# The flag of the weights behind the sum of the gate logits, three more low parts on ScalarE and Pool, and sums at the end moved forward

## The chip, the cores and the metric

The kernel runs on 1 core of one Trainium2 chip. The metric is the device time of one execution in microseconds: 616.71 us before the change (median of 3 runs, 616.56 to 619.94).

## What is computed

Clustered attention (2 batches, 8 heads, 768 tokens, 64 dimensions; a query sees only keys of its own cluster), then two mixture-of-experts layers over its 1536 tokens of 512 dimensions, each with 8 experts of 1024 hidden units and one expert per token. The first layer has a capacity per expert, the second an output gate on top. The layers, cut to what matters here:

```python
logits = x @ w_gate
e_idx = np.argmax(logits, axis=1)                    # one expert per token
gate_w = softmax(logits)[arange(N), e_idx]
eom = 1.0 / (1.0 + np.exp(-(x @ w_output_gate)))     # layer 2 alone
for e in range(E):
    mask = e_idx == e                                # layer 1: at most `capacity` tokens
    h = np.maximum(x[mask] @ w1[e], 0.0)
    out[mask] = gate_w[mask, None] * eom[mask, e, None] * (h @ w2[e])
```

## The kernel before

One program runs attention (0 to about 290 us), layer 1 (to about 460 us) and layer 2. The experts of a layer are ordered by how many tokens they have, and each place in this order (a rank) has a fixed number of rows: 192, 304, 208, 200, 192, 176, 168, 120 in layer 1. The work is cut into units, one per rank, and two for a layer's first rank: units 0 to 8 are layer 1, units 9 to 17 layer 2 (unit 9 has 256 rows, unit 17 has 88). What a unit does is written in the class MoE; `run` (L1079) puts the instructions of all engines into one order by hand, and each engine works its own queue in that order.

A unit: its tokens are gathered by an indirect DMA from Pool (`gather`), transposed on TensorE (`entry`), multiplied by the first weights (`mm1`, 8 steps f) and by the second (`mm2`, 4 steps d). Products are made from pairs of float16: a value is a high part and a low part, and three products are added. For the weights ScalarE makes the high part `wh` from the loaded `raw`, and VectorE the low part `wl` (`split`, two halves for each chunk of 1 MB; the finished low part frees `raw` for the next load, which SyncE issues). For the hidden layer ScalarE makes `hh` from the PSUM tile, and VectorE the low part `hl`. The table `FP` (L751) names the steps f of a unit in which `hl` is made otherwise: ScalarE runs once more over the PSUM tile into `hr` in float32, and Pool subtracts `hh` from it. For more than 128 rows there is one buffer `hr`, for up to 128 there are two halves. The PSUM tiles of `mm1` and `mm2` rotate over three banks. In some units of layer 2 (unit 9 among them) `mm2_by_token` multiplies the other way round (`pz`, L1000).

Each pass of VectorE over weights also sums its result into `fl`; the sum over a rank is `flt`, and a matmul with ones spreads it (`rank_ok`, L1035), from which VectorE makes `okr`: 1 if all weights are finite. `okr` marks a rank's tokens as valid.

The exit of a unit runs beside the next unit, one step of a Python generator ahead of each f or d. In layer 1 (`exit1`, L1657): the first step sums the gate logits of the unit on TensorE (`pq`), then the flag (`rank_ok` into another column of the same PSUM tile `pq`), then ScalarE copies `pq` to `lt`. The second step multiplies `lt` by `sel` into the last columns of `pq` and transposes the unit's output (`back`, tile `pyo`). The third (in unit 8, the last of the layer, still the second) makes `vbk` from `okr` on Pool and the logits `lg` on VectorE. The tile `yt`, into which ScalarE copies the results of `mm2`, has one buffer: the next unit's first copy waits for the transposes `pyo` of the unit before. The exits of several units form a group; at its last unit `routed` (L1726) chooses experts, gates and places, writes the tokens for layer 2, and in the last group builds the order of the experts and the gather indices of layer 2.

At the very end VectorE adds up the lost tokens of both layers (`lost1`, `lost2`), a matmul with ones spreads the sum, and with the counts beyond the ranks (`nov1`, `nov2`) it gives the number of rounds of a general path, which is 0 here. A register load and a branch on it end the program (L1911 to L1924).

Of the kernel before, what the change touches and what calls it, by code (L numbers as in the profile page):

```python
# [8 lines left out]
F32 = mybir.dt.float32  # L9
# [3 lines left out]
ALU = mybir.AluOpType  # L13
AX = mybir.AxisListType
# [710 lines left out]
class MoE:  # L725
# [23 lines left out]
    FX = 1  # L749
    FB = 0  # L750
    FP = {0: (2, 3, 4, 5, 6, 7), 5: (1, 3, 5), 7: (5, 7), 8: (1, 2, 5, 6), 9: (3, 4)}  # L751
    FY = 7
    SA = (1, 1, 1, 0, 1, 0, 0, 0, 0, 1, 1, 1)
    SB = (1, 1, 1, 1, 1, 1, 1, 1, 1, 1, 1, 1)
# [554 lines left out]
def tile_kernel(tc, q, k, v, centroids, wg1, w11, w12, cap_in, wg2, wog2, w21, w22, out,  # L1309
                prof1=(192, 304, 208, 200, 192, 176, 168, 120), prof2=(392, 272, 224, 192, 160, 128, 120, 88),  # L1310
                head1=128, head2=256, cut2=5, by_token=(0, 3, 5), group1=((0, 1), (2, 3), (4, 5), (6, 7, 8)), seq1=(1, 2, 3, 4, 5, 6, 7), seq2=(1, 6, 2, 5, 3, 4, 7), dbg=None):
    nc = tc.nc
    P = 128
    B, NP, _, S = q.shape
    NT, DM = out.shape
    E = wg1.shape[1]
# [6 lines left out]
    A1, A2 = (sum(len(t) for _, t in u) for u in (units1, units2))  # L1323
    S1 = sum(prof1)
    with ExitStack() as ctx:
        ctx.enter_context(tc.manual_schedule())
        const = ctx.enter_context(tc.tile_pool(name="const", bufs=1))
# [4 lines left out]
        R = Routing(tc, const, E)  # L1332
# [15 lines left out]
        lost1, lost2, tok2 = c32("lost1", A1), c32("lost2", A2), c32("tok2", A2)  # L1348
# [4 lines left out]
        if True:  # L1353
# [68 lines left out]
            keep = {}  # L1422
# [206 lines left out]
            s2 = Stage(units2, x2d, w21, w22, sws[1])  # L1629
            M = MoE(tc, mctx, ident, R, XW, DM, (s1, s2), ps_t)  # L1630
# [9 lines left out]
        def back(ys):  # L1640
            ps = []
            for i, yT in enumerate(ys):
                n = yT.shape[2]
                p = M.ps_t.tile([P, 512], F32, tag="t", name="pyo")
                for c in range(4):
                    nc.tensor.transpose(p[:n, c * P:(c + 1) * P], yT[:, c, :], ident)  # L1646
                ps.append(p)
            return ps

        fin = {}  # L1650
# [6 lines left out]
        def exit1(unit, ys):  # L1657

            group = of[id(unit)]
            ns, gs, u = unit.tiles, unit.gt, unit.u  # L1660
            t0 = group[0].first
            T = sum(len(x.tiles) for x in group)
# [10 lines left out]
            pq = M.ps_g.tile([P, 512], F32, tag="g", name="pq")  # L1673
            for c in range(4):
                nc.tensor.matmul(pq[32 * c:32 * c + 32, :N], wgc[:, c, :], unit.y[:, c, :N], start=True, stop=True)
            M.rank_ok(unit, pq[:, 511 - 2 * E * len(ns):])
            lt = M.sm.tile([P, max(prof1)], F32, tag="e1lt", name="lt", bufs=1)
            nc.scalar.copy(lt[:, :N], pq[:, :N])
            yield
# [2 lines left out]
            for i, n in enumerate(ns):  # L1682
                nc.tensor.matmul(pg[:n, 2 * E * i:2 * E * (i + 1)], lt[:, o:o + n], sel, start=True, stop=True)
                o += n
            xo = [M.xo.tile([P, XW], F32, tag="xo", name="xo") for _ in ns]
            xos += zip(xo, ns)
            ps = back(ys)
# [190 lines left out]
        def exit2(unit, ys):  # L1878
            t0, ns, gs, u = unit.first, unit.tiles, unit.gt, unit.u
# [6 lines left out]
                nc.gpsimd.memset(ls, 0.0)  # L1886
            tk = M.sm.tile([P, T], I32, tag="tk", name="tk")
            M.rank_ok(unit)
            ps = back(ys)
            if unit.xo:  # L1890
                nc.vector.tensor_reduce(ls, unit.ls, axis=AX.X, op=ALU.add)
# [16 lines left out]
        s2.units[-1].last = True  # L1908
        M.run(task)
        lim1, nov1, lim2, nov2 = keep["lim"], keep["nov"], fin["lim"], fin["nov"]  # L1910
        nov = const.tile([P, 1], F32, name="nov")  # L1911
        nl = const.tile([P, 2], F32, name="nl")
        nc.vector.tensor_reduce(nl[:, 0:1], lost1, axis=AX.X, op=ALU.add)
        nc.vector.tensor_reduce(nl[:, 1:2], lost2, axis=AX.X, op=ALU.add)
        nc.vector.tensor_tensor(nl[:, 0:1], nl[:, 0:1], nl[:, 1:2], op=ALU.add)
        pc = M.ps_g.tile([P, 512], F32, tag="g", name="plost")
        nc.tensor.matmul(pc[:, :1], R.ones, nl[:, 0:1], start=True, stop=True)
        nc.vector.tensor_tensor(nov, nov1, nov2, op=ALU.add)
        nc.vector.tensor_tensor(nov, nov, pc[:, :1], op=ALU.add)
        novi = const.tile([P, 1], I32, name="novi")  # L1920
        nc.vector.tensor_scalar_add(novi, nov, 127.0)
        nc.vector.tensor_single_scalar(novi, novi, 7, op=ALU.arith_shift_right)
        mctx.close()
        nt = nc.values_load(novi[0:1, 0:1], min_val=0, max_val=NT // P)  # L1924
# [47 lines left out]
```

## Time and profile before

| | us |
|---|---|
| median of 3 runs (lowest, highest) | 616.71 (616.56, 619.94) |
| the profiled execution | 615.39 |
| its span, first to last instruction | 613.5 |
| TensorE (PE) busy | 565.1 (92%) |
| TensorE weight loads (PEld) busy | 466.1 (76%) |
| VectorE (DVE) busy | 466.1 (76%) |
| ScalarE (ACT) busy | 421.3 (69%) |
| GpSimd (POOL) busy | 215.4 (35%) |

The profile shows one execution of the program. Times are microseconds from the start of the span, and L with a number is a line of the kernel. An instruction's idle time before it is given in brackets with the instruction that ended the wait; idle time of an engine that isn't the bottleneck costs nothing by itself. The chain that ended last is followed back from the last instruction, at each step to what released it.

### The profile page before, as it was taken

To read this page: it belongs to the slowest core of one execution; us is meant where nothing else is said; L and a number is where in the kernel's file an instruction comes from. 1 tells how busy PE (TensorE), PEld (TensorE's weight loads), DVE (VectorE), ACT (ScalarE), POOL (GpSimd) and SP (SyncE) were. 2 spreads that over 40 slices of the span, in tenths; PEclk is the share of its full clock that TensorE was granted. 3 is DMA by queue.
4 is the path that set the end of the run, shared out by engine and by line. 5 is a ranking of instruction groups with operands and counts; after the bars stand their busy time and mean duration, and the time that the engine had idled before them with its cause. 6 is when DMAs were issued, how large, how long until landed. Compare 5 with 4: busy or idle time off the path is not lost.

```text
span 613.5 us, 14527 instructions
## 1 busy us (share of the span) xinstructions
PE 565.1 (92%) x5428; PEld 466.1 (76%) x5428; DVE 466.1 (76%) x1186; ACT 421.3 (69%) x901; POOL 215.4 (35%) x426
## 2 busy tenths in 40 slices
PE   6899999998999998988899999997998999999993
PEld 2666767676767676657778998996887988999992
DVE  5867686778989676868586788789778666989881
ACT  4766666776676668963585787875864576969781
POOL 8702020202341110115634355624624523263441
PEclk9899999999999999999899999999999999999997
DMA  5879482747409881522466765976973657999930
GB/s 145 212 217 283 123 176 88 169 110 153 146 22 241 247 242 35 178 70 107 150 219 236 244 208 201 306 246 194 326 234 89 235 181 245 316 305 312 318 114 21
DMA packets 75920, 117.55 MB, mean 192 GB/s; under 512 B 10906, under 2 KB 43802, under 8 KB 75843
## 3 DMA queue, kind: packets, MB, share of 16 engines
q1 hardware_dynamic: 72419, 106.76, 58.3%
q0 software_dynamic: 3264, 9.72, 4.7%
q8 instruction: 45, 0.74, 0.5%
q14 instruction: 32, 0.26, 0.1%
q10 hardware_dynamic: 160, 0.07, 0.0%
HBM read 84.28 MB, written 12.87 MB: 158 GB/s over the span
## 4 chain that ended last, share of the span: by engine, by line
PE 61%; DVE 17%; ACT 12%; issue 4%; DMA 3%; SPq 1%; ACTq 0%; POOL 0%; DVEq 0%
PE ph L950 15%; PE py L1025 13%; PE av L280 9%; PE pss L238 7%; PE ppt L268 6%; PE pz L1000 3%; DVE nm L246 3%; DVE wl L847 3%; ACT wh L840 3%; ACT pe L254 2%; PE pyo L1646 2%; PE pxt L927 2%; ACT pt L270 1%; ACT xo L1700 1%; DVE hl L962 1%
## 5 line engine op out<-in xcount | busy, mean ns | idle before, releaser
L847 DVE SCALAR_TENSOR_TENSOR wl<-raw,sw,wh 128x1024 f16<-128x1024 f32 x128 | 163.5, 1284 | 17.9 <-ACT wh L840 16.8
L840 ACT ACTIVATE wh<-raw,sw 128x1024 f16<-128x1024 f32 x128 | 146.0, 1148 | 2.5 <-DMA x<-ot 2.4
L246 DVE TENSOR_REDUCE nm<-pss 128x1 f32<-128x768 f32 x96 | 91.5, 953 | 41.2 <-PE pss L238 37.6
L254 ACT ACTIVATE pe<-pss,nm 128x768 f32<-128x768 f32 x96 | 87.1, 907 | 24.2 <-DVE nm L246 24.2
L950 PEld LDWEIGHTS <-wh 128*128 128x128 f16 x1152 | 87.7, 99 | 15.4 <-issue 10.9
L238 PE MATMUL pss<-y,x 128*128 128x384 f32 x384 | 93.6, 365 | 4.8 <-ACT pe L254 3.2
L268 PE MATMUL ppt<-ident,pe 128*128 128x128 f32 x576 | 80.4, 275 | 3.3 <-ACT pt L270 1.4
L238 PEld LDWEIGHTS pss<-y,x 128*128 128x128 f32 x384 | 63.2, 190 | 25.2 <-issue 13.2
L270 ACT COPY pt<-ppt 128x384 f32<-128x384 f32 x128 | 57.9, 482 | 29.4 <-PE ppt L268 29.1
L268 PEld LDWEIGHTS ppt<-ident,pe 128*128 128x128 f32 x576 | 69.2, 142 | 8.9 <-ACT pt L270 2.3
L1025 PEld LDWEIGHTS <-wh 128*128 128x128 f16 x960 | 73.2, 100 | 3.4
L950 PE MATMUL ph<-xh,wh 128*128 128x192 f16 (+14 forms) x576 | 67.2, 240 | 8.6 <-DVE hl L962 6.2
L280 PE MATMUL av<-pt,v 128*64 128x384 f32 x384 | 68.8, 494 | 0.0
L950 PE MATMUL ph<-xl,wh 128*128 128x192 f16 (+14 forms) x576 | 67.3, 240 | 0.2 <-issue 0.2
L950 PE MATMUL ph<-xh,wl 128*128 128x192 f16 (+14 forms) x576 | 67.3, 240 | 0.0
L952 ACT ACTIVATE hh<-ph 128x128 f16<-128x128 f32 (+14 forms) x144 | 44.5, 315 | 27.1 <-PE ph L950 25.8
L962 DVE SCALAR_TENSOR_TENSOR hl<-ph,hh 128x192 f16<-128x192 f32 (+14 forms) x127 | 41.1, 336 | 24.4 <-ACT hh L952 22.8
L1025 PE MATMUL py<-hh,wh 128*128 128x192 f16 (+13 forms) x480 | 47.3, 241 | 0.5 <-ACT hh L952 0.3
L1025 PE MATMUL py<-hl,wh 128*128 128x192 f16 (+13 forms) x480 | 46.9, 240 | 0.2 <-DVE hl L962 0.2
L950 PEld LDWEIGHTS <-wl 128*128 128x128 f16 x576 | 45.5, 99 | 1.9
L1025 PE MATMUL py<-hh,wl 128*128 128x192 f16 (+13 forms) x480 | 46.7, 241 | 0.0
L280 PEld LDWEIGHTS av<-pt,v 128*64 128x64 f32 x384 | 24.8, 136 | 28.4 <-issue 28.1
(326 smaller groups left out, 865.3 us busy)
## 6 DMA issues: line engine op xcount, KB each, us to landing
raw<-in_moe_w SPq DMA_DIRECT2D x64, 1024.0 KB, 5.9
y<-kh SPq DMA_DIRECT2D x31, 192.0 KB, 4.0
x<-qh SPq DMA_DIRECT2D x30, 192.0 KB, 4.6
q<-in_q SPq DMA_DIRECT2D x8, 384.0 KB, 4.8
k<-in_k SPq DMA_DIRECT2D x8, 384.0 KB, 5.0
x<-ql SPq DMA_DIRECT2D x16, 192.0 KB, 3.3
v<-in_v SPq DMA_DIRECT2D x8, 384.0 KB
out<-zt SPq DMA_DIRECT2D x1, 3072.0 KB
```

The lines of the kernel that those rows point to most:

```text
L238: nc.tensor.matmul(p[:, hf, :W], xx[:, c * P:(c + 1) * P], yy[:, hf * W:(hf + 1) * W], start=a, stop=o)
L246: nc.vector.tensor_reduce(nm, p[:, :, :W], axis=AX.XY, op=ALU.max, negate=True)
L254: nc.scalar.activation(pe, p[:, :, :W], AF.Exp, bias=d["nm", c, j], scale=1.0, accum_out=d["sm"][:, c, j:j + 1])
L268: nc.tensor.transpose(p[:, kc * P:(kc + 1) * P], pe[:, kh, kc * P:(kc + 1) * P], ident)
L270: eng(pt[:, kh * HALF:(kh + 1) * HALF, (c % HALF) * P:(c % HALF + 1) * P], p.rearrange("p (a b) -> p a b", a=HALF))
L280: nc.tensor.matmul(p[j * D:(j + 1) * D, :W], d["v"][:, j, kc, :], d["pt", hf, j][:, kc, :], start=(kc == 0), stop=(kc == C - 1))
L840: nc.scalar.activation(hi[:, :, s], x[:, :, s], AF.Copy, scale=sw)
L847: nc.vector.scalar_tensor_tensor(lo[:, :, s], x[:, :, s], sw, hi[:, :, s], op0=ALU.mult, op1=ALU.subtract, accum_out=fl)
L950: nc.tensor.matmul(p[:, :N], w[:, c, fs], x[:, c, :N], start=(k == 0), stop=(k == 11))
L952: nc.scalar.activation(hh[:, f, :N], p[:, :N], AF.Relu)
L962: nc.vector.scalar_tensor_tensor(hl[:, f, :N], p[:, :N], 0.0, hh[:, f, :N], op0=ALU.max, op1=ALU.subtract)
L1025: nc.tensor.matmul(p[:, :N], w[:, f, s], x[:, f, :N], start=(k == 0), stop=(k == 23))
```

## The change

Three edits. In `exit1` the call of `rank_ok` moves from the first step (ahead of the copy `lt`) to the second (behind the products with `sel`). In `FP` unit 9 gets the steps 5, 6 and 7 in addition to 3 and 4. At the end, the sums over `lost1` and over all columns of `lost2` but the last, their sum, and the sum of both counts and 127 move into the last unit's exit, right behind its `rank_ok`; the last column of `lost2` is added by a second matmul into the same PSUM element.

```diff
--- before.py
+++ after.py
@@ -748,7 +748,7 @@
               (1, 1, 0, 1, 0, 1, 0, 1, 1, 1, 0, 1))
     FX = 1
     FB = 0
-    FP = {0: (2, 3, 4, 5, 6, 7), 5: (1, 3, 5), 7: (5, 7), 8: (1, 2, 5, 6), 9: (3, 4)}
+    FP = {0: (2, 3, 4, 5, 6, 7), 5: (1, 3, 5), 7: (5, 7), 8: (1, 2, 5, 6), 9: (3, 4, 5, 6, 7)}
     FY = 7
     SA = (1, 1, 1, 0, 1, 0, 0, 0, 0, 1, 1, 1)
     SB = (1, 1, 1, 1, 1, 1, 1, 1, 1, 1, 1, 1)
@@ -1673,7 +1673,6 @@
             pq = M.ps_g.tile([P, 512], F32, tag="g", name="pq")
             for c in range(4):
                 nc.tensor.matmul(pq[32 * c:32 * c + 32, :N], wgc[:, c, :], unit.y[:, c, :N], start=True, stop=True)
-            M.rank_ok(unit, pq[:, 511 - 2 * E * len(ns):])
             lt = M.sm.tile([P, max(prof1)], F32, tag="e1lt", name="lt", bufs=1)
             nc.scalar.copy(lt[:, :N], pq[:, :N])
             yield
@@ -1682,6 +1681,8 @@
             for i, n in enumerate(ns):
                 nc.tensor.matmul(pg[:n, 2 * E * i:2 * E * (i + 1)], lt[:, o:o + n], sel, start=True, stop=True)
                 o += n
+
+            M.rank_ok(unit, pq[:, 511 - 2 * E * len(ns):])
             xo = [M.xo.tile([P, XW], F32, tag="xo", name="xo") for _ in ns]
             xos += zip(xo, ns)
             ps = back(ys)
@@ -1886,6 +1887,15 @@
                 nc.gpsimd.memset(ls, 0.0)
             tk = M.sm.tile([P, T], I32, tag="tk", name="tk")
             M.rank_ok(unit)
+            if unit is s2.units[-1]:
+                assert T == 1
+                nl = const.tile([P, 2], F32, name="nl")
+                nov = fin["sum"] = const.tile([P, 1], F32, name="nov")
+                nc.vector.tensor_reduce(nl[:, 0:1], lost1, axis=AX.X, op=ALU.add)
+                nc.vector.tensor_reduce(nl[:, 1:2], lost2[:, :t0], axis=AX.X, op=ALU.add)
+                nc.vector.tensor_tensor(nl[:, 0:1], nl[:, 0:1], nl[:, 1:2], op=ALU.add)
+                nc.vector.scalar_tensor_tensor(nov, keep["nov"], 127.0, fin["nov"], op0=ALU.add, op1=ALU.add)
+                fin["nl"] = nl
             ps = back(ys)
             if unit.xo:
                 nc.vector.tensor_reduce(ls, unit.ls, axis=AX.X, op=ALU.add)
@@ -1908,17 +1918,11 @@
         s2.units[-1].last = True
         M.run(task)
         lim1, nov1, lim2, nov2 = keep["lim"], keep["nov"], fin["lim"], fin["nov"]
-        nov = const.tile([P, 1], F32, name="nov")
-        nl = const.tile([P, 2], F32, name="nl")
-        nc.vector.tensor_reduce(nl[:, 0:1], lost1, axis=AX.X, op=ALU.add)
-        nc.vector.tensor_reduce(nl[:, 1:2], lost2, axis=AX.X, op=ALU.add)
-        nc.vector.tensor_tensor(nl[:, 0:1], nl[:, 0:1], nl[:, 1:2], op=ALU.add)
         pc = M.ps_g.tile([P, 512], F32, tag="g", name="plost")
-        nc.tensor.matmul(pc[:, :1], R.ones, nl[:, 0:1], start=True, stop=True)
-        nc.vector.tensor_tensor(nov, nov1, nov2, op=ALU.add)
-        nc.vector.tensor_tensor(nov, nov, pc[:, :1], op=ALU.add)
+        nc.tensor.matmul(pc[:, :1], R.ones, fin["nl"][:, 0:1], start=True, stop=False)
+        nc.tensor.matmul(pc[:, :1], R.ones, lost2[:, A2 - 1:A2], start=False, stop=True)
         novi = const.tile([P, 1], I32, name="novi")
-        nc.vector.tensor_scalar_add(novi, nov, 127.0)
+        nc.vector.tensor_tensor(novi, fin["sum"], pc[:, :1], op=ALU.add)
         nc.vector.tensor_single_scalar(novi, novi, 7, op=ALU.arith_shift_right)
         mctx.close()
         nt = nc.values_load(novi[0:1, 0:1], min_val=0, max_val=NT // P)
```

## Rows read from the trace of the kernel before

**Rows 1.** The page's first line: span and instructions of the execution.

```profile
span 613.5 us, 14527 instructions
```

**Rows 2.** Busy time by stretch: us, engines (x instructions), granted clock, DMA share, GB/s.

```profile
...
410.00:430.00 20.00, 15.85 (x194) 14.58 (x192) 17.84 (x62) 13.47 (x28) 8.22 (x16) 0.96 0.61 185
550.00:570.00 20.00, 20.00 (x238) 19.06 (x236) 18.93 (x45) 18.87 (x38) 9.45 (x15) 1.00 0.93 307
```

**Rows 3.** Waits, ScalarE and TensorE, 290 to 460: us in all, times, longest.

```profile
...
ACT lt L1678 <- DVE okr L1044: 10.7, 8, 3.8
...
PE pq L1683 <- ACT lt L1678: 2.1, 3, 1.8
```

**Rows 4.** Timeline, 419 to 436: start, us, engine, line, instruction [idle before <- releaser].

```profile
...
426.98 0.31 ACT L1678 COPY lt<-pq 128x176 f32<-128x176 f32 x1 [3.76 <-DVE okr L1044]
...
427.34 0.59 PE L1683 MATMUL pq<-sel,lt 128*128 128x16 f32 x4 [1.77 <-ACT lt L1678]
...
429.35 0.30 ACT L1027 COPY yt<-py 128x168 f32<-128x168 f32 x1 [1.02 <-PE pyo L1646]
...
434.12 0.17 DVE L1710 TENSOR_SCALAR am<-am 128x2 f32<-128x2 f32 x1 [2.09 <-ACT xo L1700]
```

**Rows 5.** Busy time by stretches of 2 us behind that wait.

```profile
...
428.00:430.00 2.00, 2.00 (x15) 1.82 (x15) 1.90 (x9) 0.98 (x3) 0.38 (x1) 0.61 0.53 66
430.00:432.00 2.00, 2.00 (x18) 2.00 (x16) 1.88 (x7) 0.70 (x1) 1.70 (x2) 0.54 1.04 398
```

**Rows 6.** Timeline of Pool, 402 to 448, and one row of ScalarE.

```profile
...
420.56 0.50 POOL L960 TENSOR_TENSOR hl<-hr,hh 128x168 f16<-128x168 f32 x1
423.30 1.22 POOL L960 TENSOR_TENSOR hl<-hr,hh 128x168 f16<-128x168 f32 x1 [2.24 <-ACT hr L959]
...
438.41 0.76 POOL L908 TENSOR_SCALAR vb<-xg 128x1 f32<-128x1 f32 x1 [0.59 <-DMA xg<-x2d,idx2a]
...
442.12 0.30 ACT L959 ACTIVATE hr<-ph 128x120 f32<-128x120 f32 x1
```

**Rows 7.** Chain that ended last, 362 to 408: start, us, engine, tile, line.

```profile
...
363.34 0.31 PE pq L1042 x2
```

**Rows 8.** Timeline, 443 to 456.

```profile
...
444.46 0.21 PE L1025 MATMUL py<-hh,wh 128*128 128x120 f16 x1 [0.34 <-ACT hh L952]
...
454.31 0.26 ACT L1678 COPY lt<-pq 128x120 f32<-128x120 f32 x1 [0.56 <-DVE okr L1044]
...
455.92 0.42 DVE L962 SCALAR_TENSOR_TENSOR hl<-ph,hh 128x256 f16<-128x256 f32 x1 [0.45 <-ACT hh L952]
```

**Rows 9.** Timeline, 459 to 482: the head of layer 2.

```profile
...
462.60 0.38 ACT L959 ACTIVATE hr<-ph 128x256 f32<-128x256 f32 x1 [0.57 <-POOL hl L960]
...
464.15 0.66 POOL L960 TENSOR_TENSOR hl<-hr,hh 128x256 f16<-128x256 f32 x1
...
465.69 0.28 PE L616 MATMUL ppos<-av,rv 128*128 128x32 f16 x5
...
467.03 1.06 DVE L962 SCALAR_TENSOR_TENSOR hl<-ph,hh 128x256 f16<-128x256 f32 x3
467.49 1.03 PE L1000 MATMUL pz<-wh,hh 128*128 128x256 f16 x8 [1.52 <-DVE hl L962]
```

**Rows 10.** Chain that ended last, 440 to 482.

```profile
...
467.49 8.02 PE pz L1000 x72
```

**Rows 11.** Timeline, 592 to 614: the end.

```profile
...
603.62 0.16 DVE L1891 TENSOR_REDUCE ls<-ls 128x1 f32<-128x4 f32 x1 [0.21 <-ACT xo L977]
...
604.25 0.16 DVE L1055 TENSOR_TENSOR lost<-vb,vld 128x1 f32<-128x1 f32 x1
...
604.86 0.38 PE L1917 MATMUL plost<-nl,ones 128*128 128x1 f32 x2 [1.65 <-DVE nl L1915]
605.28 0.16 DVE L1919 TENSOR_TENSOR nov<-nov,plost 128x1 f32<-128x1 f32 x1 [0.41 <-PE plost L1917]
605.48 0.15 DVE L1921 TENSOR_SCALAR novi<-nov 128x1 int32<-128x1 f32 x1
```

## The prediction

> **What bounds the kernel now.** I read the page first: one core, one span of 613.5 us [rows 1]; with what lies around it the profiled execution took 615.39 us, and the median of the three timed runs is 616.71 us, 1.3 us more. My sum is made against the profiled execution and then subtracted from the median. A measurement of this kernel tells about 1% (6 us) from no change.
>
> Next I read the table of busy times by stretch [rows 2]. In the second layer TensorE is busy in every moment (20.00 of 20 us between 550 and 570): what is won before it shifts the rest as a whole, as long as weights keep up, and no conversion of weights on ScalarE waits for a DMA there. Late in layer 1 it is otherwise: from 410 to 430 TensorE works 15.85 of 20 us, VectorE 17.84, and TensorE's granted clock averages 0.96. So layer 1 and its seam to layer 2 are where small edits can count.
>
> Third the table of waits [rows 3]. ScalarE's copy `lt` of the gate logits (L1678) waited 10.7 us for VectorE's `okr` (L1044), in all 8 units that carry a flag, though `lt` doesn't use `okr`: both read the PSUM tile `pq`, and the two reads run one after the other in program order. `okr` stands in VectorE's queue behind low parts (`wl`) and `hl`, so the copy inherits VectorE's lateness. But TensorE waited for `lt` only three times, 2.1 us in all and 1.8 of it at one place. Most of the 10.7 us is idle time of an engine that would wait for something else next. The size of the effect has to be read place by place.
>
> **Edit 1: the flag behind the sum.** Removed: `okr` ahead of `lt`. Added: nothing; the flag's two matmul passes and `okr` move one step later, behind `sel`. On TensorE the flag now stands between `sel` and the transposes `pyo`; on VectorE `okr` moves behind one low part; on Pool `vbk`, which reads `okr`, follows later, in front of two small copies per tile. No DMA moves.
>
> The large place is unit 6's exit [rows 4]. `lt` starts at 426.98 after 3.76 us of waiting, `sel` at 427.34 after TensorE idled 1.77, and the next `yt` copy only at 429.35, since it may overwrite `yt` only after `pyo`. Behind that idle time the granted clock fell to 0.61 and 0.54 in two stretches of 2 us [rows 5], the lower of TensorE's two levels (1.2 against 2.4 GHz) for most of them: 0.39 x 2 + 0.46 x 2 = 1.7 us of TensorE's time. Without the wait TensorE is 1.77 + 1.7 = 3.5 us ahead. The chain then goes over ScalarE and VectorE, and there `am` at 434.12 shows what is late next: VectorE idled only 2.09 us before it, its own low parts ending at 432.03. So at most 2.1 us come through, not 3.5.
>
> Not all of that need stay. The gathered tokens for the first unit of layer 2 land by their own clock: Pool got the second tile at 438.41 after waiting 0.59 us for its DMA [rows 6], and the index that starts this gather doesn't come earlier. Behind it in Pool's queue stand that tile's two scalings and two `hl` subtractions of unit 8, and these free the buffer `hr` that ScalarE takes again at 442.12. Shifted by 2.1 us ScalarE would want it at 440.0; Pool is done at about 438.41 + 0.76 + 0.3 + 2 x 0.50 = 440.5. That gives back 0.5 us: I take 1.6 us, with 0 and 2.1 as bounds.
>
> At the other seven places the flag itself has to be priced: 0.31 us of TensorE [rows 7]. Where the chain runs over TensorE both before and after (the exits at 342, 363 and 404 us), 0.31 us leave one side of the main matmuls and return on the other: 0. Where TensorE stalls in the main matmuls anyway, the flag was free ahead of that stall and is paid behind it. That is so at 444.46, where the last `hh` is 0.34 us late [rows 8]: -0.3 us. At the exits near 302 and 387 the two remaining waits of [rows 3] (0.3 us together) go and 0.31 us each comes: -0.3 together, or -0.2 where a little of the flag stays hidden; I take -0.2. The last exit gains: `lt` had waited 0.56 us there with a weight conversion and a `hh` queued behind it on ScalarE, and VectorE waited 0.45 us for that `hh` at 455.92 [rows 8], right ahead of the routing of the last group. 0.45 less the pass of `okr`, now ahead of the logits (about 0.15 us): +0.3 us. Edit 1: 1.6 - 0.3 - 0.2 + 0.3 = 1.4 us; bounds -0.9 (0 at the large place and at the last exit, flags paid in full) and 2.3 (2.1 + 0.45 - 0.3).
>
> **Edit 2: f = 5, 6, 7 of unit 9 by ScalarE and Pool.** Removed from VectorE: three `hl`, 1.06 us at 467.03 [rows 9], behind the whole loading order of layer 2. The first `pz` matmul takes the PSUM bank of f = 5 and waited 1.52 us for the first of these. Added: three `hr` on ScalarE (0.38 us each) and three subtractions on Pool (0.66 us each), and one `hr` buffer that passes between them. By hand: Pool ends f = 4 at 464.81; `hr` 5 ends 465.23, which frees the bank; Pool 465.93; `hr` 6 466.35; `hh` 7 466.75; Pool 467.05; `hr` 7 467.45; Pool 468.15. TensorE is done with the inversion at 465.97 and can start `pz` there. It takes 8.02 / 72 = 0.11 us per matmul [rows 10], so it needs `hh` 7 at 465.97 + 7 x 0.11 = 466.75 and the last `hl` at 465.97 + 23 x 0.11 = 468.5. Both are just met. Gain 1.5 us, with 0.35 us to spare on Pool; I take 1.4. ScalarE's three extra passes hide in its idle time before the next `xo`. The gather for unit 10 stands behind these subtractions on Pool, but its index comes 1.06 us earlier, with the three `hl` gone from VectorE.
>
> Pool's times can stretch. One `hl` of equal shape took 0.50 us, the next 1.22 [rows 6], while VectorE ran a low part. The Trainium skill ("SBUF — State Buffer", Terms) has a rule that speaks against this edit: VectorE and GpSimd contend for one port pair, held for a whole instruction, and the loser stands still. By that rule every pass of VectorE with two operands in SBUF could hold a subtraction back, and the edit would give about 0.2 us; the row at 464.15 disagrees in part, since 0.66 us for 256 columns beside VectorE's own work is in line with 0.50 for 168. If each of the three took 1.22 us, the last would end at about 469.8 and `pz` 1.3 us later than above: 0.2 us is the lower bound, 1.5 the upper.
>
> **Edit 3: the end.** Of the last unit's sums, two reductions, an addition and the 127 move ahead of `ls`. Before, the chain ran `lost` (to 604.41), three VectorE passes, the matmul at 604.86, `nov`, then `novi` 0.20 us later [rows 11]. After, the second matmul can start 0.04 us behind `lost`: 0.41 us won, and one pass less behind it: 0.20. Against this four passes (about 0.5 us, by the three between 604.41 and 604.86) stand ahead of `ls`, where VectorE idled 0.21: -0.28. Sum 0.33 us; bounds 0.1 and 0.6 (all four hidden).
>
> **Sum.** 1.4 + 1.4 + 0.3 = 3.1 us. Span 613.5 -> 610.4, profiled execution 615.4 -> 612.3, median 616.7 -> 613.6. With all three edits at their bounds the change goes from 0.6 us slower (-0.9 + 0.2 + 0.1) to 4.4 us faster (2.3 + 1.5 + 0.6).
>
> **Rivals.**
> Given back: `lt` starts early, but the stretch after 432 us is held by the gather, or `lt` meets another wait, so that the edit doesn't do what it says. For: 0.59 us is all the slack at 438.41. Against: PE's idle 1.77 us has no other releaser in the trace. Then 1.6 us go: gain 1.5, time 615.2.
> Wider gain: the chain after 429 follows TensorE's 3.5 us and not VectorE's 2.09, because raw weights and low parts also move up. 3.1 + 1.9 = 5.0, time 611.7. Against: VectorE's three low parts there aren't moved by the edit.
> Pool as the bound at the head of layer 2: each of the three subtractions takes 1.22 us and `pz` waits for the last. For: the row at 423.30. Against: the rows at 420.56 and 464.15. Then edit 2 gives 0.2, 1.2 us less, time 614.8. The port rule of the Trainium skill ("SBUF — State Buffer", Terms) would be behind it.
> The other side: VectorE held at `okr`. In its new place it waits for a TensorE matmul that stands behind the main matmuls, `sel` and the flag, with the next weights' low part queued behind it and the next raw load behind that. If VectorE is there when `sel` starts, it loses 0.59 [rows 4] + 0.31 [rows 7] = 0.9 us, 8 times 7.2 us, and the time is 616.7 - 3.1 + 7.2 = 620.8. It decides from 0.4 us per place, if all of it reaches the end. For: VectorE is the fullest engine from 410 to 430 [rows 2]. Against: a low part stands ahead of `okr` in the new order and usually ends after the flag, and VectorE has idle time soon after at most exits.
>
> **How the numbers follow.** Forecast 0.57 (611.8 to 615.0); given back 0.15; Pool bound 0.10; wider 0.08; held at `okr` 0.10. Most of these lie within 2 us of each other, so the range is 611.0 to 617.0: outside are half the wider case, most of the other side and a little of the rest, under 2 in 10. Over 1% faster means under 610.5 us, which no case reaches in its middle: 0.04. Over 1% slower means over 622.9: 0.03. Within 1%: 0.93.
>
> **What would show it.** Edit 1: no wait of `lt` for `okr` in the table of waits; `sel` near 425.6 behind the main matmuls; the granted clock at 1.00 from 428 to 432; `am` about 2 us earlier. Wrong if VectorE's `okr` shows waits for the flag's matmul of 0.4 us and more each. Edit 2: `pz` starts with no wait for `hl`, some 3 us earlier than 467.49; wrong if it then stalls on a Pool `hl` or if Pool's subtractions take over 1 us. Edit 3: the matmul right behind `lost`, `ls` about 0.3 us after ScalarE's last sum. The whole is wrong if TensorE shows new idle time after 480 us.

## The result, and the profile after

The changed kernel took 611.11 us (median of 8 runs, 608.1 to 614.14) beside 617.16 for the kernel before (8 runs, 614.95 to 619.94): ratio 0.9895, 95% interval 0.9863 to 0.9928, that is 4.4 to 8.5 us. Two later measurements of the same two kernels gave 0.9906 (0.9871 to 0.9942) and 0.9928 (0.9900 to 0.9957); weighted by their intervals the three make 0.9912, 5.4 us, with 4.3 to 6.6 around it. I had forecast 613.6 us, 3.1 us less than before, with 0.04 for a gain of over 1%. The profiled execution has a span of 606.3 us.

**The exit of unit 6.** The busy times by stretch of the changed kernel [rows 2, 5]; columns as there, the granted clock is the third number from the end.

```profile
...
410.00:430.00 20.00, 17.62 (x232) 16.64 (x230) 19.52 (x67) 15.33 (x33) 9.12 (x17) 1.00 0.63 195
428.00:430.00 2.00, 2.00 (x31) 2.00 (x29) 2.00 (x6) 1.99 (x6) 1.28 (x2) 1.00 0.97 364
430.00:432.00 2.00, 1.84 (x32) 1.72 (x31) 1.90 (x8) 1.02 (x2) 2.00 (x2) 1.00 1.05 398
...
```

TensorE works 17.62 us of the 20 where it had worked 15.85, and both stretches of 2 us that had run at 0.61 and 0.54 are at 1.00. The timeline there [rows 4, 6, 8]:

```profile
...
421.87 0.30 ACT L1677 COPY lt<-pq 128x176 f32<-128x176 f32 x1 [0.35 <-PE pq L1675]
...
423.59 0.52 PE L1682 MATMUL pq<-sel,lt 128*128 128x16 f32 x4
...
424.04 0.38 PE L1042 MATMUL pq<-flt,ones 128*128 128x1 f32 x2
...
425.39 0.30 ACT L1027 COPY yt<-py 128x168 f32<-128x168 f32 x1 [2.17 <-PE pyo L1646]
...
430.04 0.16 DVE L1711 TENSOR_SCALAR am<-am 128x2 f32<-128x2 f32 x1
...
437.90 1.20 POOL L960 TENSOR_TENSOR hl<-hr,hh 128x120 f16<-128x120 f32 x3
...
438.34 0.27 ACT L959 ACTIVATE hr<-ph 128x120 f32<-128x120 f32 x1 [0.24 <-POOL hl L960]
...
440.67 0.21 PE L1025 MATMUL py<-hh,wh 128*128 128x120 f16 x1 [0.94 <-ACT hh L952]
...
```

`lt` waits for nothing but its own matmuls, `sel` follows the main matmuls directly, the flag (L1042) comes 0.45 us after it, and `am`, which had come at 434.12 after 2.09 us of idle time, stands right behind VectorE's low part. The table of waits (us in all, times, longest) has no `lt` behind `okr` any more [rows 3]; in its place stands what the rival "held at okr" had feared, 2.7 us in four places:

```profile
...
DVE okr L1044 <- PE pq L1042: 2.7, 4, 0.8
...
ACT lt L1677 <- PE pq L1675: 0.4, 1, 0.4
...
```

**The head of layer 2** [rows 9], timeline:

```profile
...
460.56 0.38 ACT L959 ACTIVATE hr<-ph 128x256 f32<-128x256 f32 x1 [1.23 <-POOL hl L960]
...
461.02 0.79 POOL L960 TENSOR_TENSOR hl<-hr,hh 128x256 f16<-128x256 f32 x1 [0.49 <-ACT hr L959]
...
461.54 1.30 PE L1000 MATMUL pz<-wh,hh 128*128 128x256 f16 x8
...
461.39 0.44 DVE L626 SCALAR_TENSOR_TENSOR key<-cnt,rev 128x8 f32<-128x8 f32 x1
...
462.30 0.67 POOL L960 TENSOR_TENSOR hl<-hr,hh 128x256 f16<-128x256 f32 x1 [0.49 <-ACT hr L959]
462.38 0.67 DVE L636 TENSOR_TENSOR p2RO<-rank,iota 128x64 f32<-128x64 f32 x1
...
463.67 0.51 DVE L662 TENSOR_TENSOR w<-p2RO,tab 128x32 f32<-128x32 f32 x1
...
```

`pz` starts at 461.54 without a wait. The subtractions of Pool take 0.79 and 0.67 us. **The end** [rows 11], timeline:

```profile
...
597.03 0.16 DVE L1894 TENSOR_REDUCE nl<-lost 128x1 f32<-128x16 f32 x1
...
597.38 0.15 DVE L1897 SCALAR_TENSOR_TENSOR nov<-p1nov,p2nov 128x1 f32<-128x1 f32 x1
597.45 0.15 DVE L1901 TENSOR_REDUCE ls<-ls 128x1 f32<-128x4 f32 x1
...
598.08 0.16 DVE L1055 TENSOR_TENSOR lost<-vb,vld 128x1 f32<-128x1 f32 x1
...
598.29 0.38 PE L1923 MATMUL plost<-lost,ones 128*128 128x1 f32 x2 [0.39 <-DVE lost L1055]
598.71 0.16 DVE L1925 TENSOR_TENSOR novi<-nov,plost 128x1 int32<-128x1 f32 x1 [0.48 <-PE plost L1923]
598.90 0.15 DVE L1926 TENSOR_SCALAR novi<-novi 128x1 int32<-128x1 int32 x1
```

### The profile page after: what moved, and what is told of

It is laid out like the page before. It is cut to its first block, busy times and chain, and to the rows that moved or that the text cites. A ratio compares the mean times of both kernels' runs of the same rounds, so it can differ in the third digit from the quotient of the medians.

```text
span 606.3 us, 14537 instructions
## 1 busy us (share of the span) xinstructions
PE 561.5 (93%) x5430; PEld 463.2 (76%) x5430; DVE 464.9 (77%) x1182; ACT 421.0 (69%) x904; POOL 210.1 (35%) x429
## 4 chain that ended last, share of the span: by engine, by line
PE 61%; DVE 14%; ACT 10%; DMA 5%; issue 5%; POOL 3%; SPq 1%; ACTq 0%; DVEq 0%; POOLq 0%
PE ph L950 15%; PE py L1025 13%; PE av L280 9%; PE pss L238 7%; PE ppt L268 6%; PE pz L1000 3%; DVE nm L246 3%; ACT pe L254 2%; DVE wl L847 2%; PE pyo L1646 2%; ACT pt L270 2%; PE pxt L927 1%; ACT wh L840 1%; DMA x2d<-xo 1%; DMA xg<-x2d,idx2a 1%
## 5 line engine op out<-in xcount | busy, mean ns | idle before, releaser
L950 PEld LDWEIGHTS <-wh 128*128 128x128 f16 x1152 | 86.9, 98 | 17.2 <-issue 12.8
L1025 PEld LDWEIGHTS <-wh 128*128 128x128 f16 x960 | 71.7, 98 | 5.8 <-issue 2.4
```

What stands on the lines that cost most here:

```text
L950: nc.tensor.matmul(p[:, :N], w[:, c, fs], x[:, c, :N], start=(k == 0), stop=(k == 11))
L1025: nc.tensor.matmul(p[:, :N], w[:, f, s], x[:, f, :N], start=(k == 0), stop=(k == 23))
```

## The experiments

**How the traces are compared.** The runs of one kernel scatter by up to 9 us, and an interval of five rounds is 3 to 4.7 us wide, as wide as the effects. The traces are far sharper, once one sees where the scatter is. For each trace I took the start of the same instructions of ScalarE as in the first trace of the kernel before, and noted by how much it is later (+) or earlier (-). At the first `yt` behind the first exit of layer 1 (304.4 us) the traces already differ by up to 7.3 us; from there I count from zero. At the places of the table two traces of the kernel before then agree within 0.1 us; between them single instructions differ by up to 0.7 us and come back. The six traces in which edit 1 alone acts up to 461 us spread by 0.4 us there, nearly all of it arising between 438.5 and 443 us. The names of the rows are those of the runs below (e1 to e3 are the three edits). The columns are the time in the kernel before of `yt`, `hh`, `hh`, `hh`, `yt`, `hh`, `hh`, `hh`.

```
                 304.4   396.2   438.5   442.7   452.2   460.8   480.3   595.1
again            +0.02   -0.02   -0.05   -0.06   -0.06   -0.07   -0.08   -0.08
e3_only          -0.08   -0.02   -0.02   -0.02   -0.02   -0.03   -0.03   -0.04
e1_only          +4.00   -0.22   -2.67   -2.01   -1.98   -2.52   -2.53   -2.54
e1_u6            -1.04   -0.02   -2.48   -1.81   -1.86   -1.87   -1.87   -1.88
e1_not6          +4.36   -0.22   -0.30   -0.31   -0.26   -0.80   -0.80   -0.80
okr_late         +0.86   -0.41   -2.83   -2.15   -2.34   -2.88   -2.88   -1.27
flag_own         +0.93   +0.93   +2.46   +2.45   +2.28   +1.74   +1.73   +1.73
no_e1            +0.16   -0.01   -0.03   -0.04   -0.05   -0.06   -1.48   -1.46
changed, first   -1.45   -0.23   -2.70   -2.32   -2.29   -2.83   -4.26   -4.24
after_again      +5.83   -0.18   -2.62   -1.94   -1.90   -2.43   -2.73   -2.70
after_3          +4.02   -0.19   -2.58   -1.91   -1.87   -2.41   -3.57   -3.55
end_pad          +2.57   -0.20   -2.65   -2.26   -2.22   -2.76   -4.18   -4.15
end_pad8         +1.51   -0.22   -2.69   -2.03   -2.00   -2.54   -3.73   -3.72
fp8_12           +3.21   -0.18   -2.62   -2.77   -2.61   -3.15   -3.42   -3.39
best             +0.18   -0.43   -2.90   -2.84   -3.12   -3.66   -4.82   -4.80
```

The step from 304 to 396 us is the exit near 387; from 396 to 438.5 the exit of unit 6, and to 442.7 what comes back of it; to 452 the exit near 444; to 461 the last; to 480 the head of layer 2.

**The kernel before, again** (no edit).

> The kernel before, unchanged, to see how far two traces of one program differ. If the 1.14 us by which the changed kernel leads at 295 us, ahead of every edit, and the 0.6 us that it wins around 596 us are scatter, this trace shows differences of that size against the first trace of the kernel before, at these places or others, and ratio 1.000 +- 0.003. If both traces agree within 0.2 us up to 295 us, the lead has to do with the change. The stall at the exit of unit 6 and the low granted clock behind it (0.61 and 0.54) should be there again.

Ratio 1.0015 (0.9984 to 1.0046). From 304 to 595 us it repeats the first trace within 0.08 us at the places of the table, with the stall at 427. Up to 296 us the two agree as well, within 0.15 us, and by my expectation that would tie the lead of 1.14 us to the change. The later traces say otherwise: the changed kernel itself was 4.88 and 4.01 us late at that place in its second and third trace, so the lead is scatter. The 0.6 us near 596 are scatter too: the first trace of the kernel before had lost them, this one not. Ahead of 304 us one thing recurs, the granted clock behind a pause of TensorE near 293 us. Two executions, the kernel before again and the changed one:

```profile
...
296.00:298.00 2.00, 2.00 (x34) 2.00 (x32) 2.00 (x5) 2.00 (x3) 1.86 (x3) 0.50 0.12 34
...
```

```profile
...
296.00:298.00 2.00, 1.35 (x21) 1.00 (x20) 2.00 (x8) 2.00 (x8) 1.86 (x3) 1.00 0.00 0
...
```

In one TensorE runs at the lower of its two levels there (1.2 against 2.4 GHz), in the other not. The clock stayed at 1.00 in four of the 16 traces, the first of the changed kernel, end_pad8, e1_u6 and okr_late, and these took 0.4 to 0.8 us less from 285 to 304 us than the first trace of the kernel before. The twelve others lie between 0.5 us less and 1.2 us more, so the clock is only a part of that scatter.

**Edit 1 alone, and in parts.** Of the diff, edit 1 only; then only where `s1.units.index(unit) == 6`, and only where it isn't 6 (the other exits keep the flag ahead of `lt`).

```diff
-            M.rank_ok(unit, pq[:, 511 - 2 * E * len(ns):])
             lt = M.sm.tile([P, max(prof1)], F32, tag="e1lt", name="lt", bufs=1)
...
+            M.rank_ok(unit, pq[:, 511 - 2 * E * len(ns):])
             xo = [M.xo.tile([P, XW], F32, tag="xo", name="xo") for _ in ns]
```

> Edit 1 alone. By the sum of the prediction: 1.4 us shorter (615.8 beside 617.2). By the markers of the two traces (3.1 us between 295 and 457 us): 3.1 us shorter, 614.1, of which 2.4 at the exit of unit 6, +0.5 at the last exit, -0.4 at the exit near 444. If the gain beyond the prediction is scatter of the profiled runs: 1.4 us and no more than 1.6 at the exit of unit 6 in the trace.

> Edit 1 at the exit of unit 6 alone; the other seven flags stay ahead of the logits' copy. If the place of the wait is all that counts: 2.4 us shorter in the trace behind 434 us and no gain elsewhere, and it keeps the flag hidden at the exit near 444 us, so it comes out at 2.4 to 2.8, beside 3.1 for edit 1 at all exits. By the prediction 1.6 us. If edit 1 works by what it does at all exits (waits for the flag gone everywhere), under 1 us.

> Edit 1 at the seven other exits, with unit 6 as before. By the prediction -0.2 us, that is 0.2 us longer. By the traces of edit 1 alone 0.9 us shorter: 0.14 at the exit near 302 us, 0.20 near 387, 0.0 near 342, 363, 404 and 444, 0.54 at the last. The stall at 427 us and the low granted clock behind it stay.

Ratios 0.9966 (0.9936 to 0.9996), 0.9987 (0.9958 to 1.0016) and 0.9998 (0.9974 to 1.0022). The traces: 2.54 us in all (1.4 by the prediction, 3.1 by the markers of the first two traces), 1.88 with unit 6 alone, 0.80 with the others alone, and 1.88 + 0.80 is 2.7. Unit 6 gives 2.46 us at 438.5 us and keeps 1.79 at 442.7. What takes 0.67 back is seen in the timeline of the kernel with edit 1 at unit 6 alone:

```profile
...
437.84 0.65 POOL L908 TENSOR_SCALAR vb<-xg 128x1 f32<-128x1 f32 x1 [0.62 <-DMA xg<-x2d,idx2a]
...
438.81 1.21 POOL L960 TENSOR_TENSOR hl<-hr,hh 128x120 f16<-128x120 f32 x3
...
439.25 0.27 ACT L959 ACTIVATE hr<-ph 128x120 f32<-128x120 f32 x1 [0.52 <-POOL hl L960]
...
```

Pool waits 0.62 us for the second gathered tile to land, its `hl` subtractions stand behind that, and ScalarE waits 0.52 us for the `hr` buffer that they free. This is the give-back of the prediction, at its place and near its size (0.5). The other exits: 0.20 near 387, nothing measurable near 342, 363, 404 and 444, and 0.54 at the last. For the exit near 302 I give no number: between 301 and 304 us the traces move by -0.25 to +0.24 us, and by +0.22 where nothing was changed there.

**The flag in a tile of its own.** Ahead of the logits, in another PSUM tile; `lt` shares nothing with `okr`.

```diff
+            M.rank_ok(unit)
             pq = M.ps_g.tile([P, 512], F32, tag="g", name="pq")
...
-            M.rank_ok(unit, pq[:, 511 - 2 * E * len(ns):])
```

> The flag's matmul ahead of the gate logits, in a PSUM tile of its own; nothing else changed from the kernel before. The copy of the logits then has no reader of its tile to wait for. If the wait of ScalarE's copy for VectorE's flag through the shared tile is the cause, the gain at the exit of unit 6 is the same as with edit 1 (1.8 us behind 443 us), and 2.2 to 2.9 us in all. If it is the place of the flag on TensorE (0.24 us ahead of the main matmuls or behind them), the gain is under 0.5 us. If the second tile takes a buffer that another exit or the ranks need, new waits appear and it is slower.

Ratio 1.0025 (0.9999 to 1.0050); by the trace 1.73 us slower. The third expectation came true. The timeline of this kernel at unit 6:

```profile
...
428.58 0.14 DVE L1044 TENSOR_SCALAR okr<-pfl 128x1 f32<-128x1 f32 x1
...
428.77 0.82 PE L1676 MATMUL pq<-yt,wgc 128*32 128x176 f32 x8 [3.73 <-DVE okr L1044]
...
429.85 0.17 DVE L1845 TENSOR_TENSOR tab<-ppos,tab 128x32 f32<-128x32 f32 x1
...
```

By the code these tiles share two buffers, so this step is read from the order of the rows and not measured by itself. The routing's `ppos` holds one until VectorE reads it (`tab`, 429.85, behind the logits' start), so the logits must have got the flag's buffer, and they start 0.05 us behind `okr`: now TensorE itself stands still, 3.73 us, for the same VectorE. At the last exit, where no `ppos` is held, this kernel gains the same 0.54 us as edit 1 does. So it is not the moved matmul that gains there.

**Only the reading moved.** The flag's matmul stays ahead of the main matmuls, in the logits' tile; only VectorE's `okr` moves behind `lt`.

```diff
-    def rank_ok(self, u, p=None):
+    def rank_ok(self, u, p=None, part=3):
...
-        nc.tensor.matmul(p[:, :1], self.R.ones, self.flt[u.r], start=True, stop=True)
+        if part & 1:
+            nc.tensor.matmul(p[:, :1], self.R.ones, self.flt[u.r], start=True, stop=True)
+        if part == 1:
+            return
...
-            M.rank_ok(unit, pq[:, 511 - 2 * E * len(ns):])
+            M.rank_ok(unit, pq[:, 511 - 2 * E * len(ns):], 1)
             lt = M.sm.tile([P, max(prof1)], F32, tag="e1lt", name="lt", bufs=1)
...
+            M.rank_ok(unit, pq[:, 511 - 2 * E * len(ns):], 2)
             xo = [M.xo.tile([P, XW], F32, tag="xo", name="xo") for _ in ns]
```

> The flag's matmul stays where the kernel before has it, ahead of the main matmuls and in the gate logits' tile; only VectorE's reading of it (okr) moves behind ScalarE's copy. If the cause is the copy that waits for VectorE through the shared tile, this gives all that edit 1 gives, with 1.8 us at the exit of unit 6 and 0.5 at the last, 2.2 to 2.9 us in all. If the place of the flag on TensorE matters as well, it differs from edit 1 alone by up to 0.24 us at each exit: more gain where the flag had been hidden ahead of a stall (near 302, 387 and 444 us), less at the last exit. If moving the matmul was what helped, under 0.5 us.

Ratio 0.9942 (0.9911 to 0.9973). By 461 us the trace is 2.88 us ahead, beside 2.41 to 2.83 in six traces with edit 1: 1.74 at unit 6, 0.54 at the last exit, 0.41 near 387 (edit 1: 0.20) and 0.19 near 444 (edit 1: 0). So the cause is the copy's wait for VectorE, and the place of the flag on TensorE is a small price on top: about 0.2 us at an exit where the flag had been hidden. (Of its lead 1.6 us are lost between 480 and 595 us: gathered tokens landed late, and TensorE waited 1.57 us for them at 551.81. No other trace shows this loss, and nothing was changed there.) The Trainium skill ("PSUM — Partial Sum Buffer", "PSUM bank collisions raise a hardware error") says that the compiler back end's scheduler adds a dependency between any two instructions on different engines that touch the same bank and partitions, reads and writes alike. The 10.7 us of `lt` behind `okr` [rows 3] agree, two reads of one tile, and so does this kernel: with the reads the other way round `lt` waits for `okr` nowhere (three waits for the flag's matmul are left, 1.3 us).

**Edits 2 and 3 without edit 1.** The diff without its first two pieces of layer 1.

> Edits 2 and 3 without edit 1. By the prediction 1.4 + 0.3 = 1.7 us shorter, 615.4. By the markers of the two traces 1.4 + 0.5 to 1.5 = 1.9 to 2.9 us, 614.3 to 615.3. The stall at the exit of unit 6 and the clock of 0.61 and 0.54 behind it stay.

Ratio 0.9954 (0.9921 to 0.9987). The trace: nothing until 461 us, 1.42 us at 480 and to the end. The stall at unit 6 and the low clock behind it (0.73 and 0.50) are there.

**The changed kernel twice more.**

> The changed kernel, unchanged, for its size. If the traces' own sum holds (2.67 for edit 1, 1.42 for edit 2, 0.48 for edit 3, and everything else scatter ahead of 301 us and behind the last instruction): 4.6 us shorter than before, ratio 0.9926. If the first measurement's 6.05 us is right, and something beside the three edits helps: ratio 0.989 to 0.990 again. By the prediction 3.1 us, 0.9950. The trace: the shifts from 305 to 595 us are the same as in the first trace of it (4.2 us) within 0.3 us.

> The changed kernel a third time, for its size and for edit 2. In two traces with edit 2 (the first of the changed kernel and that of edits 2 and 3) the 1.42 us won at the start of pz last to the end; in two others 1.1 to 1.2 us of it are lost again at 476 to 480 us, where ScalarE takes the third xo 1.4 us after its matmul and the next unit's xh comes late. If this belongs to the chip, the trace shows one or the other by the chip; if it is chance, either. Ratio 0.990 +- 0.002 if the first two measurements are right, 0.9926 by the traces' sum.

Ratios 0.9906 and 0.9928, as told. The traces repeat edit 1 (2.43 and 2.41 us), but of edit 2 they keep 0.30 and 1.16 us, not 1.43. `pz` starts as early in all eight traces with edit 2, at 465.81 or 465.82 us counted in the time of the kernel before; the loss comes later, at the third `xo` of unit 9. The timelines of after_again and of the first trace of the changed kernel:

```profile
...
479.70 0.48 ACT L1002 ACTIVATE xo<-pz,u 128x256 f32<-128x256 f32 x1 [1.43 <-remote]
...
482.37 0.40 PE L950 MATMUL ph<-xh,wh 128*128 128x136 f16 x4 [1.47 <-ACT xh L928]
...
```

```profile
...
470.47 0.46 ACT L1002 ACTIVATE xo<-pz,u 128x256 f32<-128x256 f32 x1
...
473.61 0.40 PE L950 MATMUL ph<-xh,wh 128*128 128x136 f16 x4 [0.39 <-ACT xh L928]
...
```

ScalarE's `xo` stood still for 1.43 us, with a weight conversion and the next unit's `xh` behind it, and TensorE waited 1.47 us for `xh` where it had waited 0.39. The matmul that `xo` needs ended at 477.51 and its signal is in the trace at 479.68, 2.17 us later; TensorE itself went on. On the chip of after_again this signal was 2.17 and 2.20 us late in both kernels with edit 2, on that of after_3 1.31 us in both, and on that of no_e1 0.01 us. The kernels without edit 2 show late signals at this `xo` or the one before it too (0.67 to 1.81 us in the three on those two chips, 0.71 and 1.03 in the first trace of the kernel before), where ScalarE's work behind it had time. So edit 2 wins its 1.4 us at the start in all eight traces, and how much stays depends on a signal that I can't explain.

**Two low parts back to VectorE.** The changed kernel with f = 5 and 6 of unit 8 made by VectorE.

```diff
-    FP = {0: (2, 3, 4, 5, 6, 7), 5: (1, 3, 5), 7: (5, 7), 8: (1, 2, 5, 6), 9: (3, 4, 5, 6, 7)}
+    FP = {0: (2, 3, 4, 5, 6, 7), 5: (1, 3, 5), 7: (5, 7), 8: (1, 2), 9: (3, 4, 5, 6, 7)}
```

> The changed kernel, with the low parts of f = 5 and 6 of unit 8 made by VectorE again (ScalarE's two passes into hr and Pool's two subtractions go). If the 0.4 to 0.7 us that come back between 438 and 443 us are ScalarE waiting for Pool, held by the landing of the gathered tokens, the hh of f = 7, for which TensorE waits 0.94 us there, comes 0.57 us earlier and the kernel gains 0.2 to 0.6 us (less where VectorE's low part of the weights is late then). If VectorE is the bound there, 0 or a loss of up to 0.4 us.

Ratio 0.9897 (0.9859 to 0.9935), beside 0.9906 for the changed kernel in the same runs. In the trace nothing comes back between 438.5 and 442.7 us (-2.62, then -2.77), and TensorE waits 0.23 us for the last `hh` where it had waited 0.94. It is 0.7 us ahead of after_again at 461 us: the give-back was ScalarE waiting for Pool. The timed runs can't tell these two kernels apart.

**Both together.** The changed kernel, with only `okr` moved and with f = 5 and 6 of unit 8 by VectorE.

> The changed kernel, with the flag's matmul back in its first place and only okr moved behind the copy, and with f = 5 and 6 of unit 8 made by VectorE. By the traces 0.4 to 0.7 us shorter than the changed kernel for unit 8, and 0 to 0.5 us for the flags: 0.4 to 1.2 us in all, ratio 0.988 to 0.989. If Pool had no part in the give-back at 438 to 443 us, the same as the changed kernel.

Ratio 0.9909 (0.9877 to 0.9942), beside 0.9928 for the changed kernel in the same runs: 0.3 us between the medians, which these runs can't tell apart. The traces of the two differ by 1.25 us at 595 us (4.80 and 3.55), every piece at its expected place.

**Edit 3 alone, and the load behind it.** Edit 3 only; then the changed kernel with 3 or 8 further passes over `novi`, which shift by nothing.

```diff
         nc.vector.tensor_single_scalar(novi, novi, 7, op=ALU.arith_shift_right)
+        for _ in range(8):
+            nc.vector.tensor_single_scalar(novi, novi, 0, op=ALU.arith_shift_right)
```

> Edit 3 alone. By the prediction 0.3 us shorter. By the traces 0.48 us in the chain from the last yt to novi, and some 0.45 us more in the load of novi, which takes 0.52 us if it begins while Pool's last scatter is in hand and about 1.0 us behind it: 0.5 to 0.95 us, ratio 0.9985 to 0.9992, which the timed runs can hardly tell from 1; the chain's 0.48 us and the load's time are read from the trace. Nothing changes ahead of the last unit's okr.

> The changed kernel with three more passes of VectorE over novi behind its shift, 0.57 us: they shift by nothing and the output is the same. In the traces so far the load of novi took 0.51 to 0.55 us where it began while Pool's last scatter was still in hand (all six traces with edit 3, and two without), and 0.94 to 1.02 us where it began 0.36 us behind the scatter's end (the other five without edit 3). If the start of the load decides, it takes 0.9 to 1.0 us here, and edit 3 is worth its 0.48 us and some 0.45 more. If something else in edit 3 shortens it, it stays at 0.51 to 0.55 us. If the scatter itself starts late in this execution (at 2.7 us or more behind the last yt, as in three of the traces), the load falls into it either way and nothing is told apart.

> The changed kernel with eight more passes of VectorE over novi behind its shift (they shift by nothing), 1.5 us, so that the load of novi begins behind the end of Pool's last scatter, whether this starts at 2.0 or at 2.7 to 3.1 us behind the last yt. If the start of the load decides, it takes 0.9 to 1.0 us. If something else in edit 3 shortens it, it stays at 0.51 to 0.55 us.

Edit 3 alone: ratio 1.0009 (0.9982 to 1.0037), which says nothing about half a microsecond. With three passes the ratio is 0.9961 (0.9905 to 1.0016); the kernel with eight passes was run once, for its trace. From the last `yt` (on VectorE) to the end of `novi` its trace has 2.86 us, the kernel before 3.34: 0.48 us. The load of `novi` into the engines' registers follows. Records of that one line, in the kernel before, with edit 3 alone and with eight passes:

```profile
...
L1924 POOLq TENSOR_LOAD <-novi x1: 1022/1022/1022, 605.9 to 605.9; - x1
...
```

```profile
...
L1927 POOLq TENSOR_LOAD <-novi x1: 517/517/517, 605.4 to 605.4; - x1
...
```

```profile
...
L1930 POOLq TENSOR_LOAD <-novi x1: 510/510/510, 604.8 to 604.8; - x1
...
```

(Durations in ns, smallest, median, largest.) The load took 0.96 to 1.02 us in five of the seven traces without edit 3 and 0.51 or 0.52 in all nine with it. My reading, that a load behind Pool's last scatter takes 1 us, fell with the eight passes: there it begins 1.4 us behind the scatter's end and takes 0.51. With three passes nothing was told apart, since the scatter itself came late. What the 16 traces leave is narrower: in all five traces with a load of about 1 us it began 1.38 or 1.39 us after the scatter had begun; at 0.13 to 0.91 us after it, and at 2.42, it was fast. Edit 3 brings the start from 1.38 to 0.91 us. So it gives 0.48 us in the chain, and 0.46 more in an execution whose load would have taken 1 us, as in five of the seven traces. From the end of `novi` to the end of the span it is 7.70 us in the kernel before and 7.21 with edit 3 alone, so the load's time reaches the end. What the load meets there stays open.

## Why the prediction was too small

**Unit 6: right, in mechanism and nearly in size.** Forecast 2.1 us of TensorE's 3.5 coming through, and 0.5 given back over Pool and `hr`: 1.6. Six traces with edit 1 everywhere and unit 8 as before show 2.39 to 2.47 coming through, above the bound of 2.1, and 1.72 to 2.09 kept. Of the part above the bound about 0.2 us is in VectorE's third low part: it starts 1.89 us earlier than before (430.73 to 428.84), where the low part ahead of it starts 1.70 earlier, which is what the traces differ by there anyway. The two rivals about this place were wrong: the stretch is not held altogether, and TensorE's 3.5 us, which are there (its matmuls of 432.17 start at 426.93, 5.24 us earlier less 1.70), don't come through.

**The other exits: the step that failed.** I priced the flags at -0.3 (444), -0.2 (302 and 387) and +0.3 (the last exit), -0.2 in all. Measured without 302: 0, +0.2 and +0.54, over 0.7 in all, so edit 1 gave 2.4 to 2.8 us in place of 1.4. Near 387 I read TensorE's wait from the bracket of `sel`, some 0.2 us. But the bracket counts from the modelled end of the matmul before, which reaches into the wait. Counting from start to start, in the kernel before and then with edit 1:

```profile
...
386.27 0.96 PE L1025 MATMUL py<-hl,wh 128*128 128x192 f16 x8
...
387.41 0.53 PE L1683 MATMUL pq<-sel,lt 128*128 128x16 f32 x4 [0.18 <-ACT lt L1678]
...
387.78 1.07 PE L1646 MATMUL pyo<-ident,yt 128*128 128x128 f32 x8
...
```

```profile
...
390.25 0.96 PE L1025 MATMUL py<-hl,wh 128*128 128x192 f16 x8
...
391.05 0.45 PE L1682 MATMUL pq<-sel,lt 128*128 128x16 f32 x4
...
391.34 0.36 PE L1042 MATMUL pq<-flt,ones 128*128 128x1 f32 x2
...
391.57 0.64 PE L1646 MATMUL pyo<-ident,yt 128*128 128x128 f32 x4
...
```

The last eight main matmuls take 0.80 us before `sel` can follow; before the change 1.14 passed. So the stall was 0.34 us. From `sel` to `pyo` it was 0.37 us and is 0.52, so the flag costs 0.15 there, not 0.31, and 0.19 is left. At 444 the flag costs 0.20 by the same count (`sel` to `pyo`, 0.51 to 0.71), but `lt` had come late there as well (445.11, after 0.70 us behind `okr`), which I had left out: from the last eight main matmuls to `sel` 0.53 us passed and now 0.42. What is left of the loss, 0.03 to 0.05 us at 452, is within the scatter. At the last exit I counted the pass of `okr` twice: it had been in VectorE's chain before, ahead of the low part (0.07 us from its start to the next), and is there after, ahead of `lg`. The chain from `hl` to `lg` went from 2.47 us (453.79 to 456.26) to 1.94, before and then after:

```profile
...
453.79 0.42 DVE L962 SCALAR_TENSOR_TENSOR hl<-ph,hh 128x256 f16<-128x256 f32 x1 [1.47 <-ACT hh L952]
...
456.26 0.22 DVE L1693 TENSOR_SCALAR lg<-pq,u 120x16 f32<-120x16 f32 x1
...
```

```profile
...
450.05 0.42 DVE L962 SCALAR_TENSOR_TENSOR hl<-ph,hh 128x256 f16<-128x256 f32 x1 [1.47 <-ACT hh L952]
...
451.59 0.42 DVE L962 SCALAR_TENSOR_TENSOR hl<-ph,hh 128x256 f16<-128x256 f32 x1
...
451.93 0.14 DVE L1044 TENSOR_SCALAR okr<-pq 128x1 f32<-128x1 f32 x1
...
451.99 0.22 DVE L1694 TENSOR_SCALAR lg<-pq,u 120x16 f32<-120x16 f32 x1
...
```

"Held at okr" did happen, 2.7 us in four places, 0.5 to 0.8 each, near 302, 342, 363 and 404 us. This is the sign that I had named for edit 1 being wrong, and it did not decide: at the last three of these places the shifts show no lost time (near 302 they can't show it).

**Edit 2: right, with two things unseen.** Forecast 1.4; 1.42 or 1.43 in three traces, 1.16 to 1.19 in three, 0.27 to 0.30 in two, in the order of the late signal above. And I expected the index of the gather for unit 10 1.06 us earlier, with three `hl` gone from VectorE. It came no earlier at all (the gather issue moved from 468.93 to 464.69, 4.24 us, with everything around it): VectorE's own passes with two operands in SBUF became longer beside Pool's subtractions. `key` (L626, 128x8) takes 0.44 us in the rows of after, `p2RO` (L636, 128x64) 0.67 and `w` (L662, 128x32) 0.51, together 1.04 us more than in the kernel before:

```profile
...
465.67 0.17 DVE L626 SCALAR_TENSOR_TENSOR key<-cnt,rev 128x8 f32<-128x8 f32 x1
...
466.39 0.22 DVE L636 TENSOR_TENSOR p2RO<-rank,iota 128x64 f32<-128x64 f32 x1
...
468.23 0.19 DVE L662 TENSOR_TENSOR w<-p2RO,tab 128x32 f32<-128x32 f32 x1
...
```

Each of the three begins while a subtraction of Pool is running and ends 0.02 to 0.08 us behind it. The Trainium skill ("SBUF — State Buffer", "SBUF: two separate sides") says that VectorE with two SBUF inputs and GpSimd exclude each other from one port pair for a whole instruction, whoever comes second standing still. The trace agrees in these three passes, with VectorE as the one that waits. I had weighed that rule for Pool alone: Pool kept its 0.67 to 0.79 us (so the rival with Pool as the bound fell), and the price fell on the other engine. It ate the 1.06 us, and as the index came no later than before, it cost no more than that.

**Edit 3: right to 0.15 us in the chain** (0.48 for 0.33, bounds 0.1 to 0.6): the four passes ahead of `ls` cost 0.12 us (from `okr` to `ls` 0.37 before, 0.49 after) and not 0.28. The load's 0.46 us are a part that no term of mine held.

**The sum.** The five traces of the changed kernel (two with passes behind its end) are 2.70 to 4.24 us ahead at 595 us, 3.7 in the mean; 0.48 and 0.33 of the load (0.85 us in the mean of the seven traces without edit 3, less 0.52) make 4.5 us by the traces. The timed runs say 5.4 (4.3 to 6.6). The prediction's 3.1 lies below both. By the traces it lacks 1.4 us: 0.9 in the small exits, 0.5 at the end (0.33 of it the load) and 0.3 at unit 6, less 0.3 that edit 2 lost to the late signal. So the failed step is the pricing of the small exits, -0.2 for over 0.7 us, with the load at the end as a term that was missing. The traces' 4.5 us lie inside the interval of the timed runs, so these don't show that anything more was gained; the first of the three measurements (1.05%) lies above the two others (0.94 and 0.72%), and that part of the distance to the forecast is chance.

## What to carry to other kernels

When one engine's copy and another engine's small read share a PSUM tile, program order decides who waits: put the read that nobody needs soon behind the copy on the critical chain. Moving the read alone was 0.2 us better at two exits here than moving its matmul too, and a tile of its own was 1.7 us worse than no change. Measure a stall from start to start of two instructions in both kernels, not by the idle time that a modelled end leaves. And where a change of half a percent is to be judged, find the place from which the traces repeat, and compare there: the shifts were good to 0.1 us (0.4 where a gather's landing or a late signal came in) where the medians were good to 2.

## What was unexpected of the hardware

The signal of a finished matmul reached ScalarE 0.01 us after its end in some executions and 2.17 us in others, alike in the kernels with edit 2 that ran on one chip, while TensorE worked on. The register load at the end took 0.51 or 1.0 us, and all loads of 1.0 us began 1.38 or 1.39 us after a scatter had begun. Behind a pause of 1.7 to 1.9 us near 293 us TensorE's granted clock fell to 0.50 in twelve of the 16 traces and stayed at 1.00 in four, whose pauses (1.77 to 1.85 us) lie among the others. And beside Pool's subtractions a pass of VectorE took 0.67 us in place of 0.22.
